# Two-level products for a part of the first layer in the last two token groups

## The chip, the core and the metric

The kernel runs on one core of a Trainium2 chip. A core has TensorE (matrix products, in the profile PE, with its weight loads as PEld), VectorE (DVE), ScalarE (ACT), GpSimd (POOL) and SyncE (SP, which here only issues transfers). The metric is the device time of one execution in microseconds (us), as the median over runs.

## The reference

The inputs are q, k, v of shape (8, 8, 576, 64) and two weight matrices, w1 (512 x 2048) and w2 (2048 x 512). All is float32.

```python
q_s, k_s = softmax(q, over the last axis), softmax(k, over the sequence)
kv = einsum('bhsd,bhse->bhde', k_s, v)
x = einsum('bhsd,bhde->bhse', q_s, kv)      # to (8, 576, 512)
u = x + real(fft(fft(x, over the sequence), over the 512))
un = (u - mean(u)) / sqrt(var(u) + 1e-6)    # over the 512
out = u + maximum(un @ w1, 0) @ w2
```

By far the most work lies in the last line, the two layers.

## The kernel before

**Groups and orders.** The 8 x 576 tokens are cut into nine groups of 512. Groups 0 to 7 take 512 tokens of one batch each, and group 8 takes what is left of all batches (its rows are called shared). They are done in the order 0, 1, ..., 6, 8, 7. The first is done plainly. The place in this list is called the order: order 6 is group 6, order 7 is group 8, and order 8 is group 7, the last. While one group goes through its two layers, the attention, the Fourier mix and the normalisation of a later one are done in between. Beside order 6 the mix of groups 7 and 8 and the normalisation of group 8 are done, beside order 7 only the normalisation of group 7 (L1844), and beside order 8 nothing.

**Seven products for eight.** Each layer of orders 1 to 8 uses Strassen's scheme in Winograd's form: both operands are cut into 2 x 2 blocks, seven products of sums of blocks are made in place of eight, and the results are put together by additions. The products are numbered 1 to 7. `ORDER` (L80) is the order in which they are made: 1, 6, 5, 7, 2, 4, 3. Sums of the left operand's blocks are called A-sides, those of the right one's B-sides. `WA_AT`, `A_AT` and `B_AT` (L71 to L75) say at which place a product's operand is kept.

**First layer** (`up`, L1533). The weights' seven A-sides were made once, at the beginning, and lie in device memory (`w1s`, eight tensors, one for each pair of 128-wide feature blocks). A group's seven B-sides are made from the normalised tokens (`unT`), the last of them by the additions at L1396, L1400 and L1405. The layer goes in four steps j. A step takes two of the eight weight tensors and makes all seven products of them, each in four matmuls of 128 x 128 weights on 256 token columns (L1544); a float32 matmul is two instructions on TensorE. The results are collected in the three banks `ba`, `bb` and `bc` of PSUM, the memory that TensorE writes to. A bank is read before the next product adds to it: ScalarE copies the first product into s1, VectorE makes u2 = bb + s1 behind the sixth product and u3 = bb + s1 behind the seventh (L1514), and the four results are finished by VectorE (L1555) and pass through ScalarE's relu (L1551, L1556). The four finished blocks of a step are the places 0 to 3 of the second layer's left operand; `a_side` (L402) then makes places 4, 5, 2 and 6 of it by four additions, on GpSimd in orders 1 to 6 and on VectorE in orders 7 and 8. A fourth bank, `one`, serves other work in this phase (`acc`, L234).

**Second layer** (`deep_down`, L1589). Here six of the seven products are cut a second time into seven: product 1 is done whole (L1641), the others in three pairs, which are called units in the code (`UNITS`, L82), with matmuls of 128 token columns (L1671) whose results are read out at L1678. The A-sides of the second cut are made at L1617. Results are added to the residual x (in the tiles `x` and `xs`) by the function `into`, at L1621; this goes on GpSimd up to order 6 and on VectorE from order 7 (E, L1593). For the unit (5, 3) these additions stand behind the end of the layer, beside the next group's first layer. `hblock` and `hpairs` are views of the first layer's results, and `gap` names four free stretches of `big` between them. In order 8 product 4 is done whole at the end.

**Weights.** Four buffers in `big` hold weights. `used` frees one and loads the fourth next in `plan` into it (`load`, L476). A step of the first layer needs two buffers of 896 KB; the second layer reads chunks of 1 MB (w2s and w2d).

**The order of the work** is written out by hand: every step of the program has a time in arbitrary units, the steps are sorted by it (L1938), and each engine then performs its instructions strictly in that order. A wait for data stops all that is queued behind it on the same engine. Transfers are issued by SP in the same way. One unit is `UP`/56 of a first layer, where `UP` (L84) is the first layer's length; one matmul pair of 256 columns is one unit.

## Time and profile before

| | us |
|---|---|
| median of 3 runs | 1006.51 |
| lowest and highest run | 1006.36 and 1007.84 |
| span of the profiled execution | 1006.6 |
| TensorE busy in it | 995.6 |
| VectorE, ScalarE, GpSimd busy | 718.6, 493.2, 442.9 |

For the profiled execution there is only its span, from the first to the last instruction; nothing is told of what lies around it. Views used below: the page, with busy times, groups of instructions and transfers; the stretches, which give each engine's busy time between two moments; the chain of work that ended last, in order of time; and the instructions of one engine in order of time. In a row of the last, the first two numbers are the start and the length in us; then stand the engine, the line in the code, the operation, what is written and read, and in brackets how long the engine was idle before it and what ended that. A line such as L1678 stands for all instructions issued from it, so groups of different products share it. A weight load is PEld. 128x512 is 128 partitions by 512 elements.

### The profile page before, as it was taken

What the parts mean: (1) busy time and instruction counts of PE and PEld (TensorE: products, weight loads), DVE (VectorE), ACT (ScalarE), POOL (GpSimd) and SP (SyncE); (2) the same over time, 40 slices, a digit from 0 to 9 for tenths busy, and PEclk for the clock granted to TensorE, in tenths of its full rate; (3) what the DMA queues carried; (4) which work ended last, traced back from release to release, by engine and by line L of the source; (5) the groups of instructions that cost most, each with busy time, mean ns of one, the idle gap of its engine ahead of it and who ended that gap; (6) DMA issues with size and microseconds to landing.
All of it is one profiled execution on the core that took longest, in us unless ns stands there. A gap on an engine that the chain in (4) does not pass through costs nothing.

```text
span 1006.6 us, 19808 instructions
## 1 busy us (share of the span) xinstructions
PE 995.6 (99%) x7562; PEld 855.7 (85%) x7562; DVE 718.6 (71%) x1356; ACT 493.2 (49%) x1277; POOL 442.9 (44%) x445
## 2 busy tenths in 40 slices
PE   8999999999999999999999999999999999999998
PEld 6844464888888899889988998899889998998897
DVE  6898898666765887588756877688667945685563
ACT  4585642872468228832775177625772342151200
POOL 4263420357535637664655465655646450040000
PEclk9999999999999999999999999999999999999999
DMA  9987499687989666975677577847753765674573
GB/s 300 258 281 245 158 240 346 205 243 226 342 283 272 230 230 219 266 237 210 251 220 242 206 269 237 253 174 270 231 204 135 267 213 200 224 265 172 183 256 132
DMA packets 123559, 236.37 MB, mean 235 GB/s; under 512 B 24184, under 2 KB 88440, under 8 KB 112840
## 3 DMA queue, kind: packets, MB, share of 16 engines
q1 hardware_dynamic: 123096, 234.58, 71.0%
q8 instruction: 60, 0.98, 0.4%
q14 instruction: 35, 0.29, 0.1%
q10 hardware_dynamic: 288, 0.26, 0.1%
q0 software_dynamic: 80, 0.26, 0.1%
HBM read 199.94 MB, written 39.06 MB: 237 GB/s over the span
## 4 chain that ended last, share of the span: by engine, by line
PE 87%; DVE 7%; ACT 3%; DMA 1%; issue 1%; SPq 0%; POOL 0%; DVEq 0%; POOLq 0%
PE bb L1544 16%; PE ba L1544 11%; PE bc L1544 11%; PE bb L1671 10%; PE ba L1671 7%; PE bc L1671 7%; PE bb L1641 5%; PE bc L1479 2%; PE bb L1760 2%; PE two L840 2%; PE one L755 2%; PE two L1207 1%; PE two L1264 1%; PE ba L1479 1%; PE bc L1760 1%; PE ba L1760 1%
## 5 line engine op out<-in xcount | busy, mean ns | idle before, releaser
L1544 PE MATMUL bb<-unT,big 128*128 128x256 f32 x768 | 183.3, 380 | 0.0
L1544 PEld LDWEIGHTS bb<-unT,big 128*128 128x128 f32 x768 | 144.8, 190 | 20.7 <-DVE u L1514 0.7
L1556 ACT ACTIVATE big<-big 128x512 f32<-128x512 f32 x96 | 59.8, 629 | 147.6 <-DVE big L1555 141.0
L1544 PE MATMUL ba<-unT,big 128*128 128x256 f32 x512 | 123.9, 382 | 0.0
L1544 PE MATMUL bc<-unT,big 128*128 128x256 f32 x512 | 121.5, 380 | 0.1
L817 ACT ACTIVATE qT<-q 32x128 f32<-32x128 f32 x384 | 117.9, 307 | 5.9 <-DVE q L807 0.8
L1544 PEld LDWEIGHTS bc<-unT,big 128*128 128x128 f32 x512 | 96.9, 190 | 13.7 <-DVE big L1555 0.5
L1544 PEld LDWEIGHTS ba<-unT,big 128*128 128x128 f32 x512 | 95.5, 190 | 13.9 <-issue 0.5
L1514 DVE TENSOR_TENSOR u<-bb,s 128x512 f32<-128x512 f32 x66 | 45.2, 685 | 85.0 <-PE bb L1544 66.5
L1671 PE MATMUL bb<-big 128*128 128x128 f32 x848 | 103.8, 276 | 0.2 <-DVE u L1678 0.2
L1671 PEld LDWEIGHTS bb<-big 128*128 128x128 f32 x848 | 98.9, 192 | 1.0 <-DVE u L1678 1.0
L1390 POOL COPY unT<-unT 32x256 f32<-32x256 f32 x98 | 42.0, 428 | 90.2 <-DVE unT L1382 85.9
L1621 POOL TENSOR_TENSOR x<-x,big 128x512 f32<-128x512 f32 x45 | 60.9, 1368 | 46.0 <-DVE big L1678 19.7
L1617 DVE TENSOR_TENSOR big<-big 128x512 f32<-128x512 f32 x98 | 79.9, 842 | 0.0
L1671 PE MATMUL ba<-big 128*128 128x128 f32 x640 | 79.0, 276 | 0.0
L1671 PEld LDWEIGHTS ba<-big 128*128 128x128 f32 x640 | 75.0, 192 | 0.8
L1390 ACT COPY unT<-unT 32x256 f32<-32x256 f32 x126 | 50.7, 402 | 31.3 <-DVE unT L1382 29.5
L804 POOL TENSOR_TENSOR q<-q,qm 128x512 f32<-128x512 f32 x24 | 25.8, 1073 | 88.2 <-DVE qm L799 53.1
L405 POOL TENSOR_TENSOR big<-big 128x512 f32<-128x512 f32 x24 | 30.4, 1268 | 68.4 <-ACT big L1556 68.4
L1641 PE MATMUL bb<-big 128*128 128x256 f32 x256 | 58.3, 379 | 0.0
L1555 DVE TENSOR_TENSOR big<-bc,u 128x512 f32<-128x512 f32 x64 | 44.0, 688 | 17.3 <-PE bc L1544 16.4
L1641 PEld LDWEIGHTS bb<-big 128*128 128x128 f32 x256 | 48.0, 190 | 6.1
(336 smaller groups left out, 1917.9 us busy)
## 6 DMA issues: line engine op xcount, KB each, us to landing
big<-w2d SPq DMA_DIRECT2D x67, 1024.0 KB, 4.6
big<-w1s SPq DMA_DIRECT2D x64, 896.0 KB, 4.7
big<-w2s SPq DMA_DIRECT2D x16, 1024.0 KB, 4.8
big<-in_w_dram SPq DMA_DIRECT2D x21, 512.0 KB, 6.0
w2d<-big SPq DMA_DIRECT2D x42, 256.0 KB, 6.5
kb<-in_kT_dram SPq DMA_DIRECT2D x28, 320.0 KB, 7.8
q<-in_q_dram SPq DMA_DIRECT2D x28, 256.0 KB, 6.0
vt<-in_v_dram SPq DMA_DIRECT2D x84, 80.0 KB, 2.7
```

Source lines behind the costliest of these rows:

```text
L405: e1.tensor_tensor(out=to(4), in0=at(2), in1=at(3), op=ALU.add)
L817: nc.scalar.activation(to[t, i * Q:i * Q + Q], one, ACT.Exp)
L1390: copy(to, of)
L1514: plus = lambda t: V.tensor_tensor(out=temp(t), in0=box["bb"][:], in1=box["s1"][:], op=ALU.add)
L1544: nc.tensor.matmul(bank()[:, i, :], lhsT=w[:, WA_AT[m], k * P:(k + 1) * P], rhs=self.unT[g][:, B_AT[m], k, :], start=first and i == 0 and ...
L1555: steps = [(0, lambda: V.tensor_tensor(out=hp(i), in0=bank()[:], in1=u()[:], op=ALU.add)), (0.8, lambda: nc.scalar.activation(hp(i), hp(i) ...
L1556: (0.8, lambda: nc.scalar.activation(hp(i), hp(i), ACT.Relu))]
L1617: e.tensor_tensor(out=to(o), in0=to(x), in1=to(y), op=op)
L1621: E.tensor_tensor(out=x, in0=x, in1=tile(m), op=ALU.add)
L1641: nc.tensor.matmul(box[name][:, i, :], lhsT=h[p][:, A_AT[m], i * P:(i + 1) * P], rhs=self.stream[n][:, p, :], start=p == 0 and (m != 1 or ...
L1671: nc.tensor.matmul(box[place[n]][:, i, :], lhsT=own(m)(A_AT[n])[:, f, :], rhs=w[:, r // 2, r % 2 * P:r % 2 * P + P], start=first and f == ...
L1760: nc.tensor.matmul(bank()[:, i, :], lhsT=h[p][:, A_AT[m], i * P:(i + 1) * P], rhs=w[:, p, :], start=first and i == 0 and p == 0, stop=p == ...
```

## The change

In orders 7 and 8 some of the seven first-layer products are themselves cut a second time into seven: the second and third in order 7, and the second, third and fourth in order 8 (`WIDE`). Such a product is done for all four steps j at once, by `wide_unit`: seven products of four matmuls on 128 token columns, one matmul for each step. The text calls this a two-level unit.

For it the raw blocks of the weights are loaded again, by seven transfers during the second layer of order 6 (`wide_load`), into tiles that the attention and the Fourier mix no longer need (`kb`, `F`, `ft`, `vt`, and buffers of `q` and `qT`). To let one transfer take several pairs, the eight tensors `w1s` become one. The four A-side sums of 128x512 are made once for both orders: for the second product on VectorE in the second layer of order 6, for the third and fourth on GpSimd in the first layer of order 7 (`wide_sums`). The four B-side differences of 128x128 of each unit are made into `gap`, on GpSimd in order 7 and on VectorE in order 8.

The first layer's steps then have the products 1, 6, 7, 5 and, in order 7, 4. Step j = 0 comes first, then the two-level units, then steps 1 to 3. The seventh goes to the bank `one`, and the fourth of order 7 is added to the seventh's in the same bank behind the reading of u3. What a unit yields stays in places 5 (second), 6 (third) and 4 (fourth) of the left operand and is merged with the steps' own results: VectorE adds the second's to the first product's bank; GpSimd adds the third's and u2, and the fourth's and u3, in advance; for step 0, which is already read out by then, GpSimd adds them afterwards (`late`), followed by the relu. Of the four A-sides of a step, GpSimd now makes two and VectorE two, and VectorE all of the last step.

In the second layer of order 7 the additions behind unit (5, 3) go to GpSimd in place of VectorE, and within unit (2, 4) the A-sides of 4 are made ahead of those of 2. `ups` gives the new lengths to the written-out times.

```diff
--- before.py
+++ after.py
+SHORT = (1, 6, 7, 5)
+UNIT, WIDE_AT = 7.2, {2: 5, 3: 6, 4: 4}
+WIDE = {B - 1: (2, 3), B: (2, 3, 4)}
...
-        self.w1s = [d.tile([P, 7, HD], F32, tag=f"w1s{p}", name=f"w1s{p}", bufs=1) for p in range(NP)]
+        self.w1c = d.tile([P, NP, 7, HD], F32, tag="w1s", name="w1s", bufs=1)
+        self.w1s = [self.w1c[:, p] for p in range(NP)]
+        self.wide = {}
         self.w2s = d.tile([7, P, NP, HD], F32, tag="w2s", name="w2s", bufs=1)
...
-        base, e = self.base[order], V if order >= B - 1 else nc.gpsimd
+        base, e = self.base[order], nc.gpsimd
+        if order >= B - 1:
+            return self.wide_up(order, g)
...
+    def wide_load(self, m):
+        self.wide[m], pairs = self.wide_places(m)
+        for i, t in enumerate(pairs):
+            p = NP // 2 * (1 - i)
+            raw = self.w1c[:, p:p + NP // 2, WA_AT[m], :]
+            if t is not None:
+                self.nc.sync.dma_start(t, raw)
+                continue
+            for k in range(2):
+                self.nc.sync.dma_start(self.wide[m][2 * i + k], raw[:, :, k * P:(k + 1) * P])
+    def wide_sums(self, m, e, *times):
+        def make(o, x, y, op):
+            w = self.wide[m]
+            e.tensor_tensor(out=w[o], in0=w[x], in1=w[y], op=op)
+        some = (4, 2, 3, ALU.add), (5, 4, 0, ALU.subtract), (2, 0, 2, ALU.subtract), (6, 1, 5, ALU.subtract)
+        return [(t, lambda a=a: make(*a)) for t, a in zip(times, some)]
+    def wide_unit(self, g, m, e, *at_sums):
+        nc, V = self.nc, self.nc.vector
+        box, sums = {}, {}
+        some = self.gap(m - 2)
+        raw = lambda i: self.unT[g][:, B_AT[m], i // 2, i % 2 * P:i % 2 * P + P]
+        b_at = lambda i: raw(i) if i in (0, 2, 3) else some[:, (4, 1, 5, 6).index(i), :]
+        to = lambda i: self.hblock(WIDE_AT[m], i % 2, 1 - i // 2)
+        place = {1: "ba", 2: "ba", 6: "bb", 4: "bb", 5: "bc", 3: "bc", 7: "one"}
+        def minus(o, x, y):
+            e.tensor_tensor(out=b_at(o), in0=raw(x), in1=raw(y) if y < 4 else b_at(y), op=ALU.subtract)
+        def product(n):
+            name, first = place[n], n in (1, 6, 5, 7, 4)
+            if n == 7:
+                box[name] = self.acc((P, D)).rearrange("p (j n) -> p j n", n=P)
+            elif first:
+                box[name] = self.ps.tile([P, 4, P], F32, tag=name, name=name)[:]
+            for j in range(4):
+                nc.tensor.matmul(box[name][:, j, :], lhsT=self.wide[m][A_AT[n]][:, j, :], rhs=b_at(B_AT[n]),
+                                 start=first and j == 0, stop=True, skip_group_check=True)
+        def temp(name):
+            t = self.work.tile([P, 2, HD], F32, tag=name, name=name, bufs=1)
+            sums[name] = t[:].rearrange("p a (e n) -> p (a e) n", n=P)
+            return sums[name]
+        def plus(out, name, t):
+            V.tensor_tensor(out=out, in0=box[name], in1=sums[t], op=ALU.add)
+        def ends(n):
+            if n == 1:
+                nc.scalar.copy(temp("s1"), box["ba"])
+            if n == 6:
+                plus(temp("u2"), "bb", "s1")
+            if n == 7:
+                plus(temp("u3"), "one", "u2")
+                plus(to(3), "bc", "u3")
+            if n == 2:
+                nc.scalar.copy(to(0), box["ba"])
+            if n == 4:
+                plus(to(2), "bb", "u3")
+            if n == 3:
+                plus(to(1), "bc", "u2")
+        steps = [(t, lambda o=o, x=x, y=y: minus(o, x, y))
+                 for t, (o, x, y) in zip(at_sums, ((4, 1, 0), (5, 3, 4), (1, 3, 1), (6, 2, 5)))]
+        for k, n in enumerate(ORDER):
+            steps += [(1.02 * k, lambda n=n: product(n)), (1.02 * k + 0.9, lambda n=n: ends(n))]
+        return steps
+    def wide_up(self, order, g):
+        nc, V, G = self.nc, self.nc.vector, self.nc.gpsimd
+        base, wide = self.base[order], WIDE[order]
+        products = [m for m in (*SHORT, 4) if m not in wide]
+        size = 2 * len(products)
+        def part(t, j, done):
+            hp = lambda i, h=self.hpairs(j, 2): h[:, :, i, :]
+            box, steps = {}, []
+            def product(m, i):
+                name = {1: "ba", 6: "bb", 7: "one", 5: "bc", 4: "one"}[m]
+                if i == 0 and m == 7:
+                    box[name] = self.acc((P, D)).rearrange("p (j n) -> p j n", n=HD)
+                elif i == 0 and m != 4:
+                    box[name] = self.ps.tile([P, 2, HD], F32, tag=name, name=name)[:]
+                w = self.stream[base + 2 * j + i]
+                for k in range(2):
+                    nc.tensor.matmul(box[name][:, i, :], lhsT=w[:, WA_AT[m], k * P:(k + 1) * P], rhs=self.unT[g][:, B_AT[m], k, :],
+                                     start=m != 4 and i == 0 and k == 0, stop=k == 1, skip_group_check=True)
+            def plus(out, name, x):
+                V.tensor_tensor(out=out, in0=box[name], in1=x(), op=ALU.add)
+            def temp(name):
+                box[name] = self.work.tile([P, 2, HD], F32, tag=name, name=name, bufs=1)[:]
+                return box[name]
+            def more(to, of, m):
+                G.tensor_tensor(out=hp(to), in0=of(), in1=hp(WIDE_AT[m]), op=ALU.add)
+            def side(e, o, x, y, op=ALU.subtract):
+                e.tensor_tensor(out=hp(o), in0=hp(x), in1=hp(y), op=op)
+            def put(dt, f, *a):
+                steps.append((t + dt, lambda: f(*a)))
+            def late(m, i):
+                put(done[m] - t, more, i, own(i), m)
+                put(done[m] - t + 1.6, relu, i)
+            def sides(t, by_pool, last):
+                put(t, side, V, 4, 2, 3, ALU.add)
+                put(t + 0.05, side, V, 2, 0, 2)
+                put(by_pool, side, V if last else G, 5, 4, 0)
+                put(by_pool + 0.1, side, V if last else G, 6, 1, 5)
+            relu = lambda i: nc.scalar.activation(hp(i), hp(i), ACT.Relu)
+            got = lambda name: lambda: box[name]
+            own = lambda i: lambda: hp(i)
+            last, own_third = j == NP // 2 - 1, j == 0 and 4 in wide
+            for k, m in enumerate(products):
+                for i in range(2):
+                    put(2 * k + i, product, m, i)
+            for n in (base + 2 * j, base + 2 * j + 1):
+                put(size - 0.5, self.used, n)
+            put(3.9, lambda: plus(temp("u2"), "bb", own(0) if j == 0 else got("s1")))
+            put(5.9, lambda: plus(hp(1) if own_third else temp("u3"), "one", got("u2")))
+            put(7.9, lambda: plus(hp(3), "bc", own(1) if own_third else got("u3")))
+            put(8.8, relu, 3)
+            if j == 0:
+                put(8.7, lambda: plus(hp(2), "bc", got("u2")))
+            else:
+                put(4.7, lambda: more(WIDE_AT[3], got("u2"), 3))
+                put(8.7, lambda: plus(hp(2), "bc", own(WIDE_AT[3])))
+            if 4 not in wide:
+                put(size - 0.1, lambda: plus(hp(1), "one", got("u2")))
+                put(size + 0.7, relu, 1)
+            if j == 0:
+                put(1.9, lambda: nc.scalar.copy(hp(0), box["ba"]))
+                for m, i in ((2, 0), (3, 2), (4, 1)):
+                    if m in wide:
+                        late(m, i)
+                t = max(done.values())
+                sides(2.6, 3.4, False)
+                return steps
+            put(1.9, lambda: nc.scalar.copy(temp("s1"), box["ba"]))
+            put(1.95, lambda: plus(hp(0), "ba", own(WIDE_AT[2])))
+            put(2.8, relu, 0)
+            if 4 in wide:
+                put(6.7, lambda: more(1, got("u3"), 4))
+                put(8.4 if last else size + 2.2, relu, 1)
+            put(9.5 if last and 4 in wide else size + 2.1 - 1.5 * last, relu, 2)
+            if last:
+                sides(size + 2.6, size + 3.4, True)
+            else:
+                sides(size + (3.95 if 4 in wide else 2.3), size + (8.3 if 4 in wide else 3), False)
+            return steps
+        t, units, done = size, [], {}
+        for k, m in enumerate(wide):
+            e, times = (V, (-5.2, -5.1, -3.1, -3.0) if k else (-3.05, -3, -1.3, -1.2)) if order == B else (
+                G, [x - t + 0.1 * i for i, x in enumerate([10.1 if k else 0.5] * 4)])
+            units += at(t, self.wide_unit(g, m, e, *times))
+            t += UNIT
+            done[m] = t + 0.5
+        steps = part(0, 0, done) + units
+        for j in range(1, NP // 2):
+            steps += part(t, j, done)
+            t += size
         return steps
...
-        def into(u, d, m):
+        def into(u, d, m, E=E):
...
-                 (5, 3): [(0.6, into, 1, 1, 5), (1.2, into, 0, 1, 5), (1.8, into, 0, 1, 3)] if last else
+                 (5, 3): [(4, into, 1, 0, 7, G), (5.5, into, 1, 1, 7, G), (7, into, 1, 1, 5, G), (8.5, into, 0, 1, 5, G), (10, into, 0, 1, 3, G)] if E is V and not last else
+                         [(0.6, into, 1, 1, 5), (1.2, into, 0, 1, 5), (1.8, into, 0, 1, 3)] if last else
...
-                for j, m in enumerate(unit):
+                for j, m in enumerate(unit[::-1] if late_second and unit == (2, 4) else unit):
...
+    ups = lambda order: len(WIDE[order]) * UNIT + 2 * (len(ORDER) - len(WIDE[order])) * (NP // 2) if order in WIDE else UP
     def timed(t, order, g):
-        b = order + 1
+        b, UP = order + 1, ups(order)
         steps = at(t, blk.up(order, g)) + at(t + UP, blk.down(g, order))
+        if order == B - 2:
+            steps += [(t + UP + dt, lambda m=m: blk.wide_load(m)) for m, dt in ((2, 4), (4, 12), (3, 25))]
+            steps += at(t + UP, blk.wide_sums(2, blk.nc.vector, 40, 41, 44, 45))
+        if order == B - 1:
+            steps += at(t, blk.wide_sums(3, blk.nc.gpsimd, 10.5, 10.6, 10.7, 10.8) + blk.wide_sums(4, blk.nc.gpsimd, 33, 34.6, 43, 44.6))
...
-        t += UP + (TWICE if order > 1 else UP)
+        t += ups(order) + (TWICE if order > 1 else UP)
```

26 lines of the change are left out of this document (23 added, 3 removed).

## The prediction

> **What bounds the kernel now.** I read the page's busy shares first, then stretches of the last 250 us, the chain of work, and each engine's instructions where two stages meet. The shares:
>
> ```profile
> span 1006.6 us, 19808 instructions
> PE 995.6 (99%) x7562; PEld 855.7 (85%) x7562; DVE 718.6 (71%) x1356; ACT 493.2 (49%) x1277; POOL 442.9 (44%) x445
> ```
>
> The stretches (us, then busy us of PE, PEld, DVE, ACT and POOL, clock, DMA share, GB/s):
>
> ```profile
> 800.00:850.00 50.00, 49.97 (x296) 45.41 (x295) 23.55 (x42) 19.20 (x39) 18.83 (x24) 1.00 0.60 208
> 900.00:950.00 50.00, 50.00 (x270) 45.03 (x269) 26.04 (x41) 9.84 (x17) 0.67 (x2) 1.00 0.57 199
> ```
>
> TensorE never rests here (50.0 us of each 50) and its clock is granted in full, 1.00. So a microsecond of product removed is gained, provided nobody makes TensorE wait. From the chain of work (start, us, what):
>
> ```profile
> 813.41 1.79 PE bc L1671 x16
> 815.20 1.73 PE ba L1544 x8
> 816.93 1.73 PE bb L1544 x8
> ...
> 863.67 6.91 PE bb L1641 x32
> ...
> 908.53 1.73 PE ba L1544 x8
> ...
> 956.88 6.91 PE bb L1641 x32
> ```
>
> The first layer of order 7 (group 8) runs from 815.20 to 863.67, that of order 8 (group 7) from 908.53 to 956.88: 28 pieces of 1.73 us each, gapless. Eight instructions of 256 columns cost 1.73 us (6.91/32 = 0.216 each); sixteen of 128 columns, in the second layer, cost 1.79 (0.112 each).
>
> **Removed and added products.** One first-layer product over all four steps j is 4 x 8 = 32 instructions, 6.91 us. Its two-level form is 7 products x 4 blocks x 2 = 56 instructions of 128 columns, 56 x 0.112 = 6.26 us (a two-level unit; 0.894 us per product). The gain is 0.65 us each; two in order 7 and three in order 8 make 5 x 0.65 = **-3.25 us**: -1.3 and -1.95.
>
> The Trainium skill ("TensorE: Matmul & The Clock Gate", LDWEIGHTS (loading the stationary operand)) gives a weight load as its columns over 1.2 in ns, an estimate of 107 ns for 128 columns, as long as the product itself. If loads were not hidden at this width, a unit would double to about 12.5 us and the change would cost 28 us; the row of 1.79 us, with a load before each product, says that they are hidden.
>
> **The chain inside a unit.** The seventh's result must become u3, and then be added to the fifth's bank, before the third may accumulate into that bank; the second and fourth lie between, 2 x 0.894 = 1.79 us. Latencies and durations from VectorE and the weight loads:
>
> ```profile
> 818.75 0.69 DVE L1514 TENSOR_TENSOR u<-bb,s 128x512 f32<-128x512 f32 x1 [2.45 <-PE bb L1544]
> 819.36 1.19 DVE L1405 TENSOR_TENSOR unT<-unT 128x512 f32<-128x512 f32 x1
> 822.14 0.69 DVE L1514 TENSOR_TENSOR u<-bb,s 128x512 f32<-128x512 f32 x1 [1.60 <-PE bb L1544]
> 822.87 0.69 DVE L1555 TENSOR_TENSOR big<-bc,u 128x512 f32<-128x512 f32 x1
> ...
> 891.72 0.41 DVE L1678 TENSOR_TENSOR u<-bb,s 128x256 f32<-128x256 f32 x1
> ```
> ```profile
> 892.18 1.86 PEld L1671 LDWEIGHTS bb<-big 128*128 128x128 f32 x16 [0.36 <-DVE u L1678]
> ```
>
> VectorE starts 0.10 after a product ends (816.93 + 1.73 = 818.66, start 818.75); the dependent add starts 0.73 after u3; TensorE follows VectorE after 0.05 (892.13 to 892.18). So 0.10 + 0.73 + 0.69 + 0.05 = 1.57 of 1.79: it fits with 0.22 us to spare, and I take 0. Cover gone, every excess is paid five times. A unit gives VectorE 5 x 0.69 = 3.45 us of work in 6.26. In order 8 four B-side differences of 128x128 join it, placed ahead of u3 or behind the add; by these rows, 0.28 to 0.79 each:
>
> ```profile
> L1129 DVE TENSOR_TENSOR eo<-eo 128x128 f32<-128x128 f32 x4 | 1.1, 281 | 0.0
> L1130 DVE TENSOR_TENSOR eo<-eo 128x128 f32<-128x128 f32 x4 | 3.2, 790 | 0.1
> ```
>
> Two sit between u2 and u3, a gap of 1.79 - 0.69 = 1.10: 0.56 fits; 1.58 is late by 0.48, beyond the spare 0.22 by 0.26, which over three units is 0.8 at most. The differences are plain rows like L1129, so 0.
>
> **The fourth in the seventh's bank (order 7).** It runs fifth, behind the fifth's 1.73 us, and needs u3 read out of the bank and the last token difference (L1405), which VectorE now does behind u3. The seventh ends at 815.20 + 3 x 1.727 = 820.38; u3 to 821.17, L1405 to 822.40 at 1.19, or 821.90 at 0.69, +0.05; the fourth is due at 815.20 + 4 x 1.727 = 822.11. Bounds 0 and 0.34; the 1.19 was measured beside GpSimd's additions, which will run there again, so **+0.3**. All other bank reuses have a whole product between.
>
> **GpSimd in order 7.** It gets the unit's B-side differences (4 before the five residual additions, 4 after), then the A-side sums of the third, the fourth's, the merges and half the A-sides:
>
> ```profile
> 813.25 1.27 POOL L1396 TENSOR_TENSOR unT<-unT 128x512 f32<-128x512 f32 x1 [0.81 <-DVE unT L1396]
> 814.48 7.19 POOL L1621 TENSOR_TENSOR x<-x,big 128x512 f32<-128x512 f32 x5
> ```
>
> and its groups by shape, with ScalarE's relu:
>
> ```profile
> L1020 POOL TENSOR_TENSOR T<-F 128x128 f32<-128x128 f32 x5 | 2.3, 458 | 0.0
> ...
> L1621 POOL TENSOR_TENSOR x<-x,big 128x512 f32<-128x512 f32 x45 | 60.9, 1368 | 46.0 <-DVE big L1678 19.7 <-issue 13.0 <-ACT big L1648 12.4
> ...
> L1579 POOL TENSOR_TENSOR big<-big 128x512 f32<-128x512 f32 x12 | 17.9, 1494 | 6.5 <-PE bc L1760 4.4 <-DMA big<-w1s 1.6
> ...
> L1556 ACT ACTIVATE big<-big 128x512 f32<-128x512 f32 x96 | 59.8, 629 | 147.6 <-DVE big L1555 141.0
> ```
>
> Free at 814.52: + 4 x 0.458 + 7.19 + 4 x 0.458 + 2 x 1.37 = 828.1 for the sum that the third's second product reads. TensorE wants it at 815.20 + 5 x 1.727 + 6.26 + 0.89 = 830.98: 2.9 us spare, so 0. The whole stage has 8 x 0.458 + 24 x 1.37 = 36.5 us of GpSimd in 47.2. The merge chain at the third unit's end (836.4) is VectorE 0.79, GpSimd 1.37, ScalarE 0.63, two A-sides on VectorE, 1.4, and u2, 0.7: free at 841.3, before the seventh of step 1 ends (836.4 + 5.18 = 841.6); u3 is read by about 842.4 and the fourth overwrites its bank at 843.3: 0.9 spare, 0. Without that cover each extra microsecond goes to TensorE once.
>
> **VectorE before it.** Four A-side sums of the second (4 x 0.69 = 2.8 us) go ahead of the token differences of group 8. There is room:
>
> ```profile
> 809.88 0.42 DVE L1678 TENSOR_TENSOR u<-bb,s 128x256 f32<-128x256 f32 x1 [2.14 <-PE bb L1671]
> ...
> 812.48 0.69 DVE L1396 TENSOR_TENSOR unT<-unT 128x512 f32<-128x512 f32 x1 [1.72 <-POOL unT L1390]
> ```
>
> Two fit into the 2.14 and two into the 1.72 us; 0. Without the gaps 2.8 us would come on top of 814.52, where the second product of the stage is due at 816.93: at most 0.4. The residual additions that go from VectorE to GpSimd at the start of order 8 (5 x 1.37) end near 912, and what they read is first written over by the third unit, after 920; the swap of the second and fourth gives the one done first 6.9 us of undivided products as cover; 0 for both.
>
> **Steps 1 to 3 of order 8.** A step is 4 x 1.73 = 6.91 us. VectorE has 7 x 0.69 = 4.8, GpSimd 4 x 1.37 = 5.5, ScalarE 5 x 0.63 = 3.1. All fit; GpSimd is nearest. Reuse of a bank comes 6.9 us after its last use, against read-outs within 2 us.
>
> **DMA and SP.** Seven wide loads (3 MB; pieces of 1 KB or 512 B) are put between the second-layer chunks of order 6, 0.3 us of SP each. Chunks are fetched three ahead, 3 x 7.15 = 21 us, and land in 4.6, so 16 us are spare; the old contents are read last before those points. 3 MB at 262 GB/s is 11.5 us spread over some 20. The first-layer weights become rows of one tensor, as w2d's are already:
>
> ```profile
> big<-w2d SPq DMA_DIRECT2D x20, 1024.0 KB, 4.6
> big<-w1s SPq DMA_DIRECT2D x16, 896.0 KB, 5.7
> ...
> 838.66 1.18 SPq L476 DMA_DIRECT2D big<-w1s  x2
> ...
> 838.00:845.00 7.00, 7.00 (x34) 6.14 (x34) 4.47 (x7) 1.84 (x3) 0.00 (x0) 1.00 0.71 262
> ```
>
> Two loads of a step, issued together at 838.66, are through by 845 (7 us x 262 GB/s = 1.83 MB, both of them): 6.3 us. In order 8 the last pair is issued one step, 6.9 us, ahead, its second half needed 0.9 later: 0, bounded by 0.5 if the stores of group 8's rows beside them add 2 us (8.3 against 7.8).
>
> **Sum.** -3.25 + 0.3 = -2.95 us against the profiled span of 1006.6, which the median of the three runs (1006.51) matches to 0.1, so the fixed remainder is nil: **1003.6 us**.
>
> **Rivals.** *VectorE in the units* (TensorE waits at each unit's third product): for it speaks the spare 0.22; against, that read-outs from banks take 0.69 in every row. With 1.19 (L1405's row) for both steps the chain is 2.57, 0.78 late, five times: 3.9, so 1007.5; from 0.35 a unit the gain sinks under 0.2%. With 0.86 apiece it is 0.1 a unit, still the forecast. *GpSimd becomes the bound of order 7* (the other side): it decides in the merge chain and the sums of the third. Slower by 0.2% needs 2.95 + 2.0 = 5 us of waiting. At the slowest group mean, 1.49, the sum is ready at 828.7, no wait; for its load to bind, the 24 operations must take (47.2 + 5 - 3.7)/24 = 2.0 us each. Then 1009. For it: the operations are in strict order, each behind a result of VectorE, and such waits add to 36.5 us of work. Against: 10.7 us free.
> The Trainium skill ("SBUF — State Buffer", Who interferes with whom) has VectorE additions with two SBUF inputs block GpSimd's reads wholly while they last. L1405's 1.19 beside the additions of 1.44 agrees; by it some 8 such additions put 5.6 us on GpSimd in this stage, which it can take, so the rival gains only a little.
> *The unit's pace is not 0.112* (the change doesn't do what it says): at 6.91/56 = 0.123 nothing is gained, 1006.8. For it: operands lie with strides of 256 columns; against: those of the second layer do too.
>
> **Chances.** Forecast 0.66 (1003.0 to 1004.4). VectorE 0.14, mostly no change (0.12). GpSimd 0.12, mostly slower (0.10). Pace 0.04, no change; a late load or something unseen 0.04, slower. Faster by over 0.2% (2 us, about what a measurement can tell) 0.68, within 0.18, slower 0.14. The range 1002.9 to 1007.5 leaves out 0.15.
>
> **What would show it.** First layer of order 7 near 47.5 us, of order 8 near 46.4; units of 6.26 us; TensorE idle only before the fourth of order 7's first step, about 0.3. Wrong if weight loads wait for VectorE at each unit's third product, for GpSimd's sum at the third unit, or if order 7's step 1 is long.

## The result, and the profile after

| | before | after |
|---|---|---|
| median (runs beside each other) | 1006.56 (18) | 1004.87 (18) |
| the same on a second occasion | 1006.83 (24) | 1004.20 (7) |
| ratio, 95% interval | | 0.9981 (0.9974 to 0.9988); second: 0.9972 (0.9961 to 0.9983) |
| span of the profiled execution | 1006.6 | 1003.0 |
| first layer of order 7 | 48.47 | 47.88 |
| second layer of order 7 | 44.86 | 44.82 |
| first layer of order 8 | 48.35 | 46.39 |
| from order 7's start to TensorE's end | 187.4 | 184.8 |

Faster by 0.2% on the first occasion and by 0.3% on the second; a ratio of 1 lies outside both intervals. The stage lengths come from the rows of the chain of work, those of after being, in parts:

```profile
814.13 1.73 PE ba L1687 x8
815.86 1.73 PE bb L1687 x8
817.58 1.74 PE one L1687 x8
819.32 0.02 issue
819.35 0.69 DVE u L1691
820.04 1.48 DVE unT L1410
821.51 0.04 issue
821.56 1.99 PE one L1687 x8
823.55 0.89 PE ba L1636 x8
...
835.16 0.94 PE bc L1636 x8
836.11 1.73 PE ba L1687 x8
...
862.01 6.91 PE bb L1845 x32
...
906.83 1.73 PE ba L1687 x8
...
932.50 1.73 PE ba L1687 x8
...
953.22 6.91 PE bb L1845 x32
```

The two-level products (L1636) run at 0.89 each without a gap, and order 8 has no wait at all. In order 7 there is one: the chain leaves TensorE at 819.32, goes through u3 and the last token difference on VectorE, and comes back at 821.56. Busy times and stretches of the same kernel (columns as in the prediction):

```profile
PE 992.3 (99%) x7682; PEld 856.7 (85%) x7682; DVE 734.3 (73%) x1382; ACT 499.0 (50%) x1287; POOL 501.2 (50%) x492
```
```profile
800.00:850.00 50.00, 49.45 (x342) 46.20 (x342) 30.48 (x50) 20.80 (x42) 39.34 (x44) 1.00 0.61 208
900.00:950.00 50.00, 50.00 (x344) 47.08 (x343) 29.27 (x53) 13.27 (x24) 20.51 (x16) 1.00 0.51 180
```

GpSimd rose from 18.8 to 39.3 us in the first stretch, and TensorE is idle for 0.55 us there, 0.52 of it in that one wait. The spans differ by 3.6 us, more than the stages; the rest lies at the program's beginning. Order 1's first layer starts at 174.8 us in the profile of before and at 173.7 in that of after (172.1 to 174.8 in all profiles of this case), and from there to order 7 it takes 640.2 us in both.

### The profile page after: what moved, and what is told of

Same layout as the page of the kernel before. It is cut to its first block, busy times and chain, and to the rows that moved or that the text cites. A ratio compares the mean times of both kernels' runs of the same rounds, so it can differ in the third digit from the quotient of the medians.

```text
span 1003.0 us, 20195 instructions
## 1 busy us (share of the span) xinstructions
PE 992.3 (99%) x7682; PEld 856.7 (85%) x7682; DVE 734.3 (73%) x1382; ACT 499.0 (50%) x1287; POOL 501.2 (50%) x492
## 4 chain that ended last, share of the span: by engine, by line
PE 85%; DVE 8%; ACT 4%; issue 1%; DMA 1%; SPq 0%; POOL 0%; DVEq 0%; POOLq 0%
PE bb L1551 11%; PE bb L1875 10%; PE ba L1551 8%; PE bc L1551 7%; PE ba L1875 7%; PE bc L1875 7%; PE bb L1845 6%; PE bc L1484 2%; PE one L1687 2%; PE bb L1965 2%; PE two L845 2%; ACT qT L822 2%; PE two L1212 1%; PE two L1269 1%; PE one L760 1%; PE ba L1484 1%
## 5 line engine op out<-in xcount | busy, mean ns | idle before, releaser
L1551 PE MATMUL bb<-unT,big 128*128 128x256 f32 x576 | 137.8, 381 | 0.0
L1551 PEld LDWEIGHTS bb<-unT,big 128*128 128x128 f32 x576 | 108.4, 190 | 15.5 <-DVE u L1519 0.5
L1875 PE MATMUL bb<-big 128*128 128x128 f32 x848 | 103.8, 276 | 0.2
L1875 PEld LDWEIGHTS bb<-big 128*128 128x128 f32 x848 | 98.9, 192 | 1.0 <-DVE u L1882 1.0
L1551 PE MATMUL ba<-unT,big 128*128 128x256 f32 x384 | 93.7, 383 | 0.0
L1551 PE MATMUL bc<-unT,big 128*128 128x256 f32 x384 | 91.2, 380 | 0.1
L1563 ACT ACTIVATE big<-big 128x512 f32<-128x512 f32 x72 | 44.7, 629 | 77.9 <-DVE big L1562 71.3
L1551 PEld LDWEIGHTS bc<-unT,big 128*128 128x128 f32 x384 | 72.5, 190 | 10.4 <-DVE big L1562 0.5
L1519 DVE TENSOR_TENSOR u<-bb,s 128x512 f32<-128x512 f32 x50 | 34.2, 684 | 64.4 <-PE bb L1551 45.9
L1551 PEld LDWEIGHTS ba<-unT,big 128*128 128x128 f32 x384 | 71.3, 190 | 10.6 <-issue 0.5
L1821 DVE TENSOR_TENSOR big<-big 128x512 f32<-128x512 f32 x98 | 79.7, 840 | 0.0
L1875 PE MATMUL ba<-big 128*128 128x128 f32 x640 | 79.0, 276 | 0.0
L1875 PEld LDWEIGHTS ba<-big 128*128 128x128 f32 x640 | 75.0, 192 | 0.8
L1395 POOL COPY unT<-unT 32x256 f32<-32x256 f32 x98 | 44.1, 450 | 48.1 <-DVE unT L1387 43.8
L410 POOL TENSOR_TENSOR big<-big 128x512 f32<-128x512 f32 x24 | 30.5, 1270 | 67.2 <-ACT big L1563 67.2
L1875 PE MATMUL bc<-big 128*128 128x128 f32 x416 | 50.7, 275 | 0.0
```

The source lines that it names most:

```text
L410: e1.tensor_tensor(out=to(4), in0=at(2), in1=at(3), op=ALU.add)
L1395: copy(to, of)
L1519: plus = lambda t: V.tensor_tensor(out=temp(t), in0=box["bb"][:], in1=box["s1"][:], op=ALU.add)
L1551: nc.tensor.matmul(bank()[:, i, :], lhsT=w[:, WA_AT[m], k * P:(k + 1) * P], rhs=self.unT[g][:, B_AT[m], k, :], start=first and i == 0 and ...
L1563: (0.8, lambda: nc.scalar.activation(hp(i), hp(i), ACT.Relu))]
L1821: e.tensor_tensor(out=to(o), in0=to(x), in1=to(y), op=op)
```

## The experiments

Line numbers in rows are those of the kernel that ran. In the changed kernel L1636 are the products of the units, L1645 their readings on VectorE and L1656 one on ScalarE, L1611 the sums of the weights' blocks, L1627 the differences of the tokens' blocks, L1687 and L1691 the undivided products and their readings, L1698 the merges, and in the second layer L1821 the sums, L1875 the products, L1882 the readings; L1551 and L1519 are the undivided products and their readings where an order is done as before, with its A-sides at L410 to L413. "Order 7" and "order 8" are the lengths of their first layers, read from the starts of their first products.

**The layout alone.** Before, with the eight weight tensors as one and nothing else.

```diff
-        self.w1s = [d.tile([P, 7, HD], F32, tag=f"w1s{p}", name=f"w1s{p}", bufs=1) for p in range(NP)]
+        self.w1c = d.tile([P, NP, 7, HD], F32, tag="w1s", name="w1s", bufs=1)
+        self.w1s = [self.w1c[:, p] for p in range(NP)]
...
```

> The kernel before with only its eight first-layer weight tensors made one tensor; no product is changed. Theory 1 (the layout costs nothing, what is missing of the gain lies in the last 200 us): same as before, within 0.3 us. Rival (the strided rows slow the stores at the beginning or the 64 loads, and eat 0.8 us of the gain all over the kernel): 0.6 to 1.0 us slower than before, and the stage marks in the first 100 us come later.

Measured: 1007.27 against 1007.03, ratio 1.0002 (0.9993 to 1.0011). Order 7 took 48.5, order 8 48.3. By the medians alone a cost of up to 1.1 us could hide in the interval, but the stages show none: order 1 starts at 172.1 us here and at 174.8 before, and from there on every stage is as long as before within 0.1 us.

**The last token difference ahead of u3.** The changed kernel with one VectorE instruction (L1410) moved between u2 and u3 in group 8.

```diff
-            put(7.5 + 18.2 + 16 * .4, combine_last)
+            put(7.5 + (17.3 if g == B else 18.2) + 16 * .4, combine_last)
```

> The changed kernel with one step moved: VectorE makes the last token difference ahead of u3 of order 7's first step instead of behind it. Theory 1 (the fourth waits for that difference, 0.7 us in the trace after, and for nothing else): the first layer of order 7 falls from 47.88 to 47.2 us and the time by 0.7, to about 1004.2. Rival (u3 is then late and takes its place, or the difference is late for another reason): 47.6 to 47.9 and no change of the time.

> The early token difference alone, once more, on the same chip and beside the same runs of the kernel before. From its first measurement: ratio 0.9967, order 7 at 47.2 us, order 8 at 46.4 us. If the 0.7 us it gains on the changed kernel is only the wait removed, the ratio stays between 0.996 and 0.9975.

Measured: 1003.27, ratio 0.9967 (0.9954 to 0.9979), and the second time 1003.86, 0.9972 (0.9961 to 0.9983). Order 7 took 47.1 both times, 0.75 less than in the changed kernel, and the wait is gone. VectorE of this kernel, instructions in order of time:

```profile
817.09 0.69 DVE L1691 TENSOR_TENSOR u<-bb,big 128x512 f32<-128x512 f32 x1 [2.23 <-PE bb L1687]
817.70 0.68 DVE L1410 TENSOR_TENSOR unT<-unT 128x512 f32<-128x512 f32 x1
818.76 0.69 DVE L1691 TENSOR_TENSOR u<-one,u 128x512 f32<-128x512 f32 x1 [0.38 <-PE one L1687]
```

The difference fits into a gap in which VectorE had nothing to do. It also takes 0.68 where it took 1.55 in the changed kernel: it starts as one of GpSimd's additions ends (817.76), and now GpSimd's next one is the longer, 1.79 in place of 1.27. This is the best version found. Against the kernel before it is faster by 0.3%; its advantage over the changed kernel is seen in the trace (0.75 us), while the intervals of the two ratios overlap.

**Order 8 alone.** Order 7 stays as before, its A-sides on VectorE.

```diff
-WIDE = {B - 1: (2, 3), B: (2, 3, 4)}
+WIDE = {B: (2, 3, 4)}
...
-        base, e = self.base[order], nc.gpsimd
-        if order >= B - 1:
+        base, e = self.base[order], V if order >= B - 1 else nc.gpsimd
+        if order in WIDE:
```

> The two-level products in order 8 alone (second to fourth); order 7 has its undivided seven products, with the transfers and sums for order 8 still beside it. Theory 1 (0.65 us for each two-level product, nothing lost): order 8 takes 46.4 us against 48.35, the whole 1.95 us less than before, 1004.6. Rival (order 8's saving is lost behind the layer, in the second layer or at the end): order 8 short but the whole less than 1.3 us faster.

Measured: 1009.98, ratio 1.0022 (1.0013 to 1.0031): slower. Order 8 has its 46.4, but order 7, which was to stay at 48.4, took 53.6. VectorE of this kernel, then GpSimd and TensorE in the same stretch:

```profile
828.13 1.23 DVE L410 TENSOR_TENSOR big<-big 128x512 f32<-128x512 f32 x1 [0.77 <-ACT big L1563]
829.39 1.64 DVE L411 TENSOR_TENSOR big<-big 128x512 f32<-128x512 f32 x1
830.95 1.75 DVE L412 TENSOR_TENSOR big<-big 128x512 f32<-128x512 f32 x1
832.81 1.56 DVE L413 TENSOR_TENSOR big<-big 128x512 f32<-128x512 f32 x1
834.30 0.68 DVE L1519 TENSOR_TENSOR u<-bb,s 128x512 f32<-128x512 f32 x1
...
845.31 0.69 DVE L410 TENSOR_TENSOR big<-big 128x512 f32<-128x512 f32 x1 [0.69 <-ACT big L1563]
```
```profile
830.45 1.71 POOL L1611 TENSOR_TENSOR q<-vt,q 128x512 f32<-128x512 f32 x1
832.12 1.71 POOL L1611 TENSOR_TENSOR T<-vt,qT 128x512 f32<-128x512 f32 x1
```
```profile
829.85 1.89 PE L1551 MATMUL bc<-unT,big 128*128 128x256 f32 x8
835.03 3.23 PE L1551 MATMUL bb<-unT,big 128*128 128x256 f32 x8 [3.29 <-DVE u L1519]
838.05 2.39 PE L1551 MATMUL ba<-unT,big 128*128 128x256 f32 x8
```

The four A-sides read both operands from SBUF (the core's memory for operands and results, as against the banks of PSUM), and GpSimd at that time made its eight sums in a row, in the same way. VectorE's additions took 1.23 to 1.75 where the same line takes 0.69 seventeen microseconds later, GpSimd's went from 1.28 to 1.71. By these rows they end in turn, GpSimd's at 832.16, VectorE's at 832.70, GpSimd's at 833.83, VectorE's at 834.37, as if each had waited for the other. TensorE waited 3.29 us for u2, which was queued behind them; most of the rest of the 5.1 us that order 7 grew by is a lower clock behind this wait (last section). Neither theory had this; the next run tests it.

**Order 8 alone, order 7's A-sides on GpSimd.** One engine then makes sums and A-sides one behind the other. The edit is against the run just shown.

```diff
-        base, e = self.base[order], V if order >= B - 1 else nc.gpsimd
+        base, e = self.base[order], nc.gpsimd
```

> Order 8 changed as a whole (second, third and fourth divided), order 7 left as before, but with the A-sides of order 7 on GpSimd as they were for the orders before it, in place of VectorE. Theory (in the run with order 8 alone VectorE's A-sides and GpSimd's eight sums, all between two operands in SBUF, held each other up, and TensorE then waited 3.3 us): with one engine doing both there is no such wait, order 7 takes 48.4 us, order 8 46.4, and the kernel is 1.95 us faster than before, ratio 0.998. Rival (GpSimd does both one behind the other and is late, or the wait has another cause): order 7 stays above 50 us and the kernel is no faster than before.

Measured: 1005.07, ratio 0.9981 (0.9972 to 0.9990). Order 7 took 48.3, order 8 46.4, so the gain is order 8's. Its waits of TensorE from 700 us on are one line (what waits, for whom, sum, times, longest):

```profile
PE bb L1875 <- DVE u L1882: 0.2, 1, 0.2
```

So it was the two engines' additions holding each other up; the A-sides on VectorE alone are not enough, since the kernel before has them there, without GpSimd's sums, and order 7 takes 48.47. The Trainium skill ("SBUF — State Buffer", Who interferes with whom) says that a VectorE instruction with two SBUF inputs contends with a GpSimd instruction that reads SBUF, and that the one that comes second blocks until the other is done; the rows agree. Three units in order 8 alone bring most of the change's gain.

**Order 7 alone.** Two units there, nothing for the fourth, and order 8 as before.

```diff
-WIDE = {B - 1: (2, 3), B: (2, 3, 4)}
+WIDE = {B - 1: (2, 3)}
...
-        base, e = self.base[order], nc.gpsimd
-        if order >= B - 1:
+        base, e = self.base[order], V if order >= B - 1 else nc.gpsimd
+        if order in WIDE:
...
-            steps += [(t + UP + dt, lambda m=m: blk.wide_load(m)) for m, dt in ((2, 4), (4, 12), (3, 25))]
+            steps += [(t + UP + dt, lambda m=m: blk.wide_load(m)) for m, dt in ((2, 4), (3, 25))]
...
-            steps += at(t, blk.wide_sums(3, blk.nc.gpsimd, 10.5, 10.6, 10.7, 10.8) + blk.wide_sums(4, blk.nc.gpsimd, 33, 34.6, 43, 44.6))
+            steps += at(t, blk.wide_sums(3, blk.nc.gpsimd, 10.5, 10.6, 10.7, 10.8))
```

> The two-level products in order 7 alone (second and third, the fourth in the seventh's bank); order 8 undivided, no transfers or sums for the fourth. Theory 1: order 7 takes 47.9 us against 48.47, 0.6 us less than before, 1005.9 (1.3 saved, 0.7 lost at the fourth). Rival (the head or the transfers cost 0.8): no faster than before.

Measured: 1007.50, ratio 1.0003 (0.9994 to 1.0012). Order 7 took its 47.9, but order 8 49.2, 0.8 more than before. Its waits of TensorE:

```profile
PE one L1687 <- DVE unT L1410: 0.5, 1, 0.5
PE ba L1551 <- DMA big<-w1s: 0.4, 1, 0.4
```

The second half of the weights of order 8's first step came late from memory; with what a wait costs besides (next run) the 0.4 is some 0.7 of the 0.8. So the kernel is no faster than before, as the rival has it, but by a load in order 8, not by the beginning. In the changed kernel this wait does not occur. Why the load took 7.0 us here, where the kernel before shows 4.4, was not settled.

**One more VectorE addition in each unit.**

```diff
                 plus(temp("u3"), "one", "u2")
+                plus(sums["u3"], "one", "u2")
                 plus(to(3), "bc", "u3")
```

> The changed kernel with one more VectorE addition (seventh plus u2, made twice) in each of the five units, between u3 and the addition into the fifth's bank. Theory (the chain inside a unit has 0.22 us to spare): the chain becomes 0.10 + 0.73 + 0.73 + 0.69 + 0.05 = 2.30 us against 1.79, so TensorE waits 0.5 us at each unit's third product, five times: 2.6 us slower than the changed kernel, about 1007.4. Rival (the chain has more room than these rows show, because the weight load and not the product waits, or the reads from the bank overlap): under 1 us slower, no waits of TensorE at a unit's third product.

Measured: 1008.04, ratio 1.0014 (1.0004 to 1.0023). The waits of TensorE have the line

```profile
PE bc L1636 <- DVE big L1645: 2.3, 5, 0.5
```

five times, 0.46 on average against 0.51 expected: the theory of the chain holds, with a spare of 0.27 (0.73 - 0.46) where 0.22 was worked out. But the two orders grew by 1.5 and 2.1 us, 3.6 in place of 2.6, 0.72 a unit. TensorE at one such place:

```profile
826.37 1.06 PE L1636 MATMUL ba<-unT,kb 128*128 128x128 f32 x8
827.26 1.06 PE L1636 MATMUL bb<-big,kb 128*128 128x128 f32 x8
828.77 1.16 PE L1636 MATMUL bc<-unT,q 128*128 128x128 f32 x8 [0.45 <-DVE big L1645]
829.76 1.06 PE L1636 MATMUL ba<-unT,F 128*128 128x128 f32 x8
```

A piece lasts 1.06 but the next one starts 0.89 later, since they overlap. Across the wait the starts are 1.51 apart, then 0.99: 0.62 and 0.10 over 0.89. So a wait of 0.45 costs 0.72: the idle time, 0.17 of overlap lost and 0.10 at the restart. (The 0.72 rests on starts alone; the ends of matmuls, and so the split, are modelled by the profile.)

**More work for GpSimd ahead of the third's sums.**

```diff
-            steps += at(t, blk.wide_sums(3, blk.nc.gpsimd, 10.5, 10.6, 10.7, 10.8) + blk.wide_sums(4, blk.nc.gpsimd, 33, 34.6, 43, 44.6))
+            steps += at(t, [s for k in range(4) for s in blk.wide_sums(3, blk.nc.gpsimd, 10.4 + 0.01 * k)] + blk.wide_sums(3, blk.nc.gpsimd, 10.5, 10.6, 10.7, 10.8) + blk.wide_sums(4, blk.nc.gpsimd, 33, 34.6, 43, 44.6))
```

(With one time given, only the first of the four sums is made.)

> The changed kernel with the first A-side sum of the third made four times more on GpSimd in order 7, ahead of the sums that the third's second product reads. Theory (in the changed kernel GpSimd's sum is ready 2.35 us before TensorE wants it, 828.34 against 830.69): 4 x 1.27 = 5.1 us more is 2.7 us too late, so TensorE waits about 2.7 us once at the second product of order 7's third unit, and the kernel is 2.7 us slower than the changed one, about 1007.5, a little more if TensorE resumes slowly. Rival (GpSimd has room because its additions wait for other things anyway): under 1 us slower.

TensorE of this kernel:

```profile
830.18 1.06 PE L1636 MATMUL ba<-unT,F 128*128 128x128 f32 x8
834.30 1.16 PE L1636 MATMUL bb<-big,cd 128*128 128x128 f32 x8 [3.07 <-POOL cd L1611]
```

The four additions took 5.4 us, and 3.07 of them were a wait, so 2.3 us were spare, as the rows of after say. Order 7 took 51.2, 3.3 more than in the changed kernel: the wait and some 0.25. The median, 1009.79 (ratio 1.0034, 1.0021 to 1.0048), is higher than the profiled execution's 1008.85: that one shows a mean granted clock of 1.000, the four others 0.997 or 0.998 and 0.9 to 3.1 us more. This fits a clock that drops behind the wait in some executions and not in others (last section), which the profile of one execution cannot show.

**The change once more.**

> The changed kernel unchanged, to measure its gain more closely. By the stage lengths of its trace (order 7 shorter by 0.6 us, order 8 by 2.0) the gain is 2.6 us, ratio 0.9974; by the medians so far it is 1.7 us, ratio 0.9983. The rest would be something outside these two stages that costs 0.9 us.

Measured: 1004.20, ratio 0.9972 (0.9961 to 0.9983); orders 7 and 8 at 47.8 and 46.4. The 2.6 us of the stages are within this interval, and those of the first measurement (1.2 to 2.6) just reach it. There is no sign of a further cost elsewhere: from order 1 to order 7 this profile too has the 640.2 us of before.

**Three units in order 7 too.** With the early difference; the fourth's sums follow the third's on GpSimd.

```diff
-WIDE = {B - 1: (2, 3), B: (2, 3, 4)}
+WIDE = {B - 1: (2, 3, 4), B: (2, 3, 4)}
...
-            e, times = (V, (-5.2, -5.1, -3.1, -3.0) if k else (-3.05, -3, -1.3, -1.2)) if order == B else (
+            e, times = (V, (-5.2, -5.1, -3.1, -3.0) if k else (-3.05, -3, -1.3, -1.2)) if order == B or k == 2 else (
...
-            steps += at(t, blk.wide_sums(3, blk.nc.gpsimd, 10.5, 10.6, 10.7, 10.8) + blk.wide_sums(4, blk.nc.gpsimd, 33, 34.6, 43, 44.6))
+            steps += at(t, blk.wide_sums(3, blk.nc.gpsimd, 10.5, 10.6, 10.7, 10.8) + blk.wide_sums(4, blk.nc.gpsimd, 11, 11.1, 11.2, 11.3))
```

In this kernel the second layer of order 7 reads a few rows of the last step ahead of their relu, so a part of group 8's output is another; the amount of work is the same.

> The kernel with the early token difference (the run before that had it), and the fourth divided in order 7 as well: its A-side sums are made on GpSimd right behind those of the third, its B-side differences on VectorE. No undivided fourth is left in order 7, so nothing waits for the seventh's bank. Theory (0.65 us for each divided product, and GpSimd in time): order 7 goes from 47.2 to 46.4 us, as order 8 has it with three units, 0.8 us in all; GpSimd's second sum of the fourth is ready near 833.4 (830.8 for the third's last, plus 2 x 1.27), wanted near 834.5. Ratio about 0.996. Rival (GpSimd is late, since VectorE's differences and these sums hold each other up): a wait of TensorE of about 1 us at the second product of the fourth's unit, and no gain over the early token difference alone.

Measured: 1012.33, ratio 1.0053 (1.0039 to 1.0066); order 7 took 53.7. GpSimd, then TensorE:

```profile
835.20 1.31 POOL L1611 TENSOR_TENSOR T<-vt,qT 128x512 f32<-128x512 f32 x1
836.47 1.31 POOL L1698 TENSOR_TENSOR big<-big 128x512 f32<-128x512 f32 x1
```
```profile
834.29 1.13 PE L1636 MATMUL bc<-unT,ZT 128*128 128x128 f32 x8 [0.57 <-DVE big L1645]
838.97 2.07 PE L1636 MATMUL ba<-unT,vt 128*128 128x128 f32 x8 [3.55 <-ACT big L1656]
840.84 1.91 PE L1636 MATMUL bb<-big,qT 128*128 128x128 f32 x8
842.54 1.52 PE L1636 MATMUL bc<-big,qT 128*128 128x128 f32 x8
```

The rival named the right engine but not the way. The late merge of the second unit (L1698) stood behind all eight sums until 837.78; its relu waited for it on ScalarE, and behind the relu, in ScalarE's written order, stood the copy (L1656) that frees the bank `ba`. TensorE waited 3.55 us for an engine that was idle, and behind the wait its clock dropped (last section). The differences of the fourth, on VectorE beside GpSimd's sums, took 0.69 to 1.34 each, so the contention that the rival names is there too.

**The same with GpSimd's sums moved into order 6**, and with the rows read behind their relu: the fourth's four sums and the third's first two (in the second kernel the fourth's alone) are made in the second layer of order 6, the fourth's differences on GpSimd. The first kernel, against the one with the early difference:

```diff
-WIDE = {B - 1: (2, 3), B: (2, 3, 4)}
+WIDE = {m: (2, 3, 4) for m in (B - 1, B)}
...
-                G, [x - t + 0.1 * i for i, x in enumerate([10.1 if k else 0.5] * 4)])
+                G, [x - t + 0.1 * i for i, x in enumerate([(0.5, 10.1, 11)[k]] * 4)])
...
-            early = 6 if last and t < n + 8 else 0 if t == 8 else t - n + 2 if i == 2 else t - n + (0 if last else 3)
+            early = 6 if last and t < n + 8 else (order[0] == 1 and E is V) if t == 8 else t - n + 2 if i == 2 else t - n + (0 if last else 3)
...
+            steps += at(t + UP, blk.wide_sums(4, blk.nc.gpsimd, 23, 23.1, 23.2, 23.3) + blk.wide_sums(3, blk.nc.gpsimd, 31.4, 31.4, 48, 48.1)[:2])
...
-            steps += at(t, blk.wide_sums(3, blk.nc.gpsimd, 10.5, 10.6, 10.7, 10.8) + blk.wide_sums(4, blk.nc.gpsimd, 33, 34.6, 43, 44.6))
+            steps += at(t, blk.wide_sums(3, blk.nc.gpsimd, 10.5, 10.6, 10.7, 10.8)[2:])
```

> Three units in order 7 again, with GpSimd's work moved: the four sums of the fourth and the first two of the third are made in the second layer of order 6, where GpSimd is idle (5.6 us near 783 to 789, 3.3 us near 796 to 800); only the third's last two sums and the differences stay in order 7. Theory (the loss with six units came from eight sums in a row on GpSimd, behind which a merge and its relu on ScalarE held a copy out of TensorE's bank): no wait of TensorE at the units, order 7 46.4 us, ratio about 0.996, 0.7 us under the kernel with the early token difference. Rival (the moved sums hold up VectorE's and GpSimd's second-layer sums in order 6, which then costs as much): order 6 longer by 0.5 us or more, no gain over 0.997.

> The same, but with all four sums of the third left in order 7, as in the changed kernel. The units begin 1.73 us earlier than there, since no undivided fourth is left, so the spare of 2.35 us that GpSimd had falls to about 0.6; in the run with six units and the same sums TensorE waited 0.3 us at that place. Theory: a wait of 0 to 0.4 us at the second product of the third's unit and nothing else, between the kernel with the early token difference and the other of this pair, ratio 0.9965. Rival (GpSimd has no room at all in order 7): over 1 us of waits there.

Measured: 1008.14 (1.0015, 1.0006 to 1.0024) and 1009.01 (1.0023, 1.0014 to 1.0032): slower. In the first kernel order 7 has no wait left and took 46.4, as its theory says. But the second layer of order 6 grew from 52.4 to 56.0 and that of order 7 from 44.8 to 46.4. VectorE in order 6 of that kernel:

```profile
785.51 1.50 DVE L1299 TENSOR_TENSOR x<-x,eo 128x257 f32<-128x257 f32 x1
786.94 1.48 DVE L1300 TENSOR_TENSOR x<-x,eo 128x255 f32<-128x255 f32 x1
788.34 0.41 DVE L1882 TENSOR_TENSOR big<-bb,s 128x256 f32<-128x256 f32 x1
```

L1299 and L1300 take 0.42 and 0.41 at this place in the kernel without these sums; reads from a bank (L1882) keep their 0.41. TensorE waited for readings behind them in three places, 3.0 us in all. The rival holds: GpSimd's idle time there was no free time, because VectorE paid for it. In the second kernel the wait expected at the third's second product did not come, and neither theory has what did: TensorE waited 0.5 us for the same ScalarE copy as in the run before, and in order 6 (55.8 us) it waited once, for 2.1 us, behind which its clock dropped (last section). The 1.6 us of order 7's second layer are the same in both kernels and lie at its start: its first sums on VectorE stand behind the last relu and take 2.37 for two, beside GpSimd's A-sides, where they take 1.47 otherwise.

## Why the prediction was right, and where it was not

- **Products: right to the hundredth.** 0.89 each; order 8 gained 1.96 for the predicted 1.95, order 7 gained 1.38 for 1.30 once its wait was gone (47.09 in the run with the early difference).
- **The chain inside a unit at 0: right.** With 0.73 more TensorE waited 0.46, which leaves 0.27 of spare for the 0.22 worked out. What an excess costs was too low: 0.27 a wait come on top.
- **The fourth in the seventh's bank, +0.3: the right place, mis-sized.** It measured 0.75, as the run without it shows. Two things were missed: VectorE's last difference took 1.55 beside GpSimd's additions, not 1.19, so that the idle time was 0.52 and not 0.34, although the difference started 0.2 us earlier than worked out; and what a wait costs besides its idle time, some 0.25.
- **GpSimd in order 7 at 0: right.** Its sum was ready at 828.34, 2.35 us ahead of the 830.69 when TensorE took it, for 2.9 predicted. (The clock times of the two profiles can't be compared, since order 7 starts 1.07 us earlier in that of after: from its start the sum took 14.2 us for the 12.9 worked out, and TensorE came to it after 16.6 for 15.8.) Work beyond the spare became a wait one for one. The rival was rightly refused, but the weight given to the two engines' contention was too low. The prediction charged it to GpSimd alone, while in the rows VectorE waits too, and TensorE behind VectorE. It decides three of the versions tried, order 8 alone and the two with sums in order 6, by some 5 us each, and the changed kernel escapes because its VectorE work beside GpSimd's sums mostly reads a bank of PSUM.
- **VectorE's sums in the gaps, the residual additions, steps 1 to 3, transfers at 0: right.** Order 7's second layer is unchanged (44.86 and 44.82), so is order 6's (52.4), and order 8 has no wait. VectorE's four sums took 0.77 to 1.31 each where 0.69 was reckoned, and still fitted. That the loads are harmless holds for the changed kernel; with order 7 alone one came 0.4 us late.
- **The fixed remainder nil: wrong.** In the profile of after the same execution has a span of 1003.0 and a time of 1004.87, and the other runs show 1.7 to 2.2. By that the profiled execution of before took some 1008.5 us (1006.6 + 1.9), 1.9 above the median, and the agreement of its span with the median was a coincidence. The sum from the median, 1006.51 - 2.95, is the same number to 0.1, so by luck the error did not touch the forecast.

The sum was -2.95 and the stages gave -2.6; the difference is the fourth's wait. The medians gave -1.7 and -2.6. The first median, 1004.87, lies 0.5 us outside the 1003.0 to 1004.4 of the forecast, the second, 1004.20, within it. Why the first gain is smaller than the stages was not found, but its interval reaches to -2.6.

## What to carry to other kernels

Price a wait of the bounding engine with more than its idle time, and look for an idle gap of the engine that it waits for before accepting it: moving one instruction ahead of another was worth 0.75 us here. When moving additions between VectorE and GpSimd, ask of each neighbour whether it reads both operands from SBUF; idle time of one engine need not be free: sums moved into it made order 6's second layer 3.7 us longer here. Where engines keep a written order, follow what stands behind each new wait, two engines on if need be.

## What was not expected of the hardware

**The granted clock after an idle stretch.** The stretches of the run with order 8 alone, around its 3.29 us wait (columns as above; the clock stands behind the five busy times):

```profile
831.00:835.00 4.00, 0.74 (x4) 0.31 (x2) 3.87 (x4) 0.00 (x0) 2.82 (x2) 1.00 0.92 291
835.00:837.00 2.00, 1.97 (x6) 1.66 (x7) 0.00 (x0) 0.00 (x0) 0.00 (x0) 0.66 0.58 134
837.00:839.00 2.00, 2.00 (x6) 1.55 (x6) 0.69 (x1) 0.00 (x0) 0.00 (x0) 0.50 0.00 0
839.00:843.00 4.00, 4.00 (x20) 3.54 (x19) 1.38 (x2) 1.30 (x3) 0.00 (x0) 0.99 0.02 4
```

And those of the run with more GpSimd work, around its wait of 3.07 us:

```profile
831.00:834.00 3.00, 0.23 (x3) 0.04 (x1) 0.07 (x1) 0.58 (x1) 2.84 (x3) 1.00 0.87 274
834.00:836.00 2.00, 1.70 (x15) 1.70 (x16) 0.44 (x1) 0.00 (x0) 2.00 (x3) 1.00 0.29 67
```

After 3.29 us the clock was granted at half for 3.4 us, and two pieces took 3.23 and 2.39 in place of 1.89: 1.8 us lost beside the wait. After the 3.55 us of the run with six units it was at half for 6.8 us. After 3.07 us it stayed at 1.00 in the profiled execution. The length of the wait alone does not decide it. The two kernels with sums in order 6 have the same wait there, the second kernel's row first:

```profile
795.97 3.63 PE L1875 MATMUL bb<-big 128*128 128x128 f32 x16 [2.14 <-DVE u L1882]
```
```profile
796.05 2.05 PE L1875 MATMUL bb<-big 128*128 128x128 f32 x16 [2.14 <-DVE u L1882]
```

In the second kernel the clock was at half for 3.4 us from 795.9 on, and the piece took 3.63; in the first it stayed at 1.00. And of the eleven executions of order 8 alone, four have a mean clock of 1.000 and took 1006.95 to 1009.38 us, the others 0.997 or 0.998 and 1009.45 to 1010.93. The Trainium skill ("TensorE: Matmul & The Clock Gate", Part 1: The HAM clock gate (the "warmup" mystery)) puts the idle window at about 3.4 us, running freely, so that where a wait falls in it may matter. The stretches at half, 3.4 and 6.8 us, are one and two such windows; but waits of 2.14 and 3.29 us, shorter than a window, were already enough here.

**Two engines' additions.** Beside each other, with both operands in SBUF, 128x512 went from 0.69 to as much as 1.75 on VectorE, 128x256 from 0.42 to 1.5, and on GpSimd 128x512 from 1.27 to as much as 1.79. The four 128x128 differences of the run with six units took 0.69 to 1.34 on VectorE, against the 0.28 of the prediction's row. Up to about 1.1 us come on top whatever the size, so small additions suffer most.
